# An attention block's forward and backward on one core: V scaled instead of K, whole 12 KB rows for V, column tiles, and score sums on the tensor engine

## Chip, cores and metric

One core of a Trainium2 chip. The metric is device time in microseconds (us) of one execution. PE is the tensor engine (matmuls), PEld its weight loads, DVE the vector engine, ACT the scalar engine, POOL and SP the two engines that issue most transfers.

## The reference

A block with one query token, 32 heads of width 192 and caches of 8192 keys and values per head, all in bf16: an adaptive layer norm, attention over the caches, an output projection, then an MLP. Forward and the gradients of it are wanted. What matters here:

```python
q = (x @ wq).reshape(B, Sq, Hq, Dh)                      # one token, Hq = 32, Dh = 192
scores = einsum('bhqd,bhkd->bhqk', q, k) * Dh ** -0.5    # 8192 keys a head
p = softmax(scores)
o = einsum('bhqk,bhkd->bhqd', p, v)
# ... output projection, MLP ...
out, vjp = jax.vjp(f, x, k_cache, v_cache, wq, wo, ...)  # the outputs include dK and dV, as large as the caches
```

K and V are 100 MB each (32 x 8192 x 192 x 2 bytes), and so are dK and dV. K is read once, V twice.

## The kernel before

Three stages. The **forward** goes through the heads; in step i it computes the scores of head i (multiply K by q, fold the 192 columns, sum) and, for head i-1 whose exponentials E are known, the matrix M = sum over keys of E * K^T [1, V], 194 columns wide. M gives o and the softmax sum Z, and spares the backward a second reading of K. K is scaled by E, in quarters of 16 key columns. V lies in a padded buffer: a column pair of keys has two columns of ones before and after it. A **middle** does the MLP. The **backward** reads V again: per half head it makes dP = V do (multiply, fold, sum), from it dS, and writes dV = E do^T (matmuls with one row, copied out by ACT) and dK = dS q^T.

J = 64 keys a partition, JH = 32, JQ = 16.

```python
    def load_v(h, t):
        vb = VB[nv[0] % NVB]
        nv[0] += 1
        nc.sync.dma_start(out=vb[:, :, 2 : 2 + PW], in_=V_hd[h][:, t * JH : (t + 1) * JH, :].rearrange("p (a b) d -> p a (b d)", b=2))
        return vb

    def dot_half(src4, vec, dst):
        prod = pp.tile([P, JH, DH], BF16, name="prod", tag="prod")
        V_.tensor_tensor(
            out=prod.rearrange("p (a b) d -> p a b d", b=2),
            in0=src4,
            in1=vec[:, None, None, :].to_broadcast([P, JH // 2, 2, DH]),
            op=ALU.mult,
        )
        w = DH
        for _ in range(3):
            w //= 2
            V_.tensor_tensor(out=prod[:, :, 0:w], in0=prod[:, :, 0:w], in1=prod[:, :, w : 2 * w], op=ALU.add)
        V_.reduce_sum(out=dst, in_=prod[:, :, 0:w], axis=AX.X)
# ... cut ...
        def scale_k(q, kb, E4, Ef):
# ... cut ...
            A_.copy(out=ks[:, :, DH:KW], in_=E4[:, j0 : j0 + JQ, :])
            V_.tensor_tensor(
                out=ks[:, 0:n, 0:DH].rearrange("p j (a b) -> p j a b", b=4),
                in0=kb[:, k0 : k0 + n, :].rearrange("p j (a b) -> p j a b", b=4),
                in1=E4[:, j0 : j0 + n, None, :].to_broadcast([P, n, DH // 4, 4]),
                op=ALU.mult,
            )
# ... cut ...
        def m_quarter(q, ks, vb, mp):
            for k in range(JQ):
                s = q == 0 and k == 0
                e = q == 3 and k == JQ - 1
                a, b = divmod((q % 2) * JQ + k, 2)
                o = 2 * b
                rhs = vb[:, a, b * (DH + 2) : b * (DH + 2) + DH + 2]
                T_.matmul(mp[:, o : o + DH + 2], lhsT=ks[:, k * KW : k * KW + P], rhs=rhs, start=s, stop=e, skip_group_check=True)
                T_.matmul(mp[:, MO + o : MO + o + DH + 2], lhsT=ks[:, k * KW + P : k * KW + 2 * P], rhs=rhs, start=False, stop=e, skip_group_check=True)
# ... cut ...
            for t in range(2):
                if i < HQ:
                    dot_half(kh[t].rearrange("p (a b) d -> p a b d", b=2), qs_bc[:, i * DH : (i + 1) * DH], S_h[:, t * JH : (t + 1) * JH])
                if i > 0:
                    pk, pv, pE4, pEf = st[i - 1]
                    for q in (2 * t, 2 * t + 1):
                        ks = scale_k(q, pk[t], pE4, pEf)
                        m_quarter(q, ks, pv[t], mp)
                if i < HQ and t == 0:
                    vh.append(load_v(i, 1))
            if i < HQ:
                E4, Ef = softmax(i, S_h)
                st[i] = (kh, vh, E4, Ef)
# ... cut ...
            for t in range(2):
                js = slice(t * JH, (t + 1) * JH)
                v = load_v(h, t)
                dP = tcol(JH, "dP")
                dot_half(v[:, :, 2 : 2 + PW].rearrange("p a (b d) -> p a b d", b=2), doh, dP)
# ... cut ...
                dSf = tcol(NAK, "dSf")
                A_.copy(out=dSf, in_=dS4[:, 0:NAK, 0])
                dK = ob.tile([P, JH, DH], BF16, name="dK", tag="o")
                for jj in range(NAK):
                    A_.activation(out=dK[:, jj, :], in_=qh, func=ACT.Copy, scale=dSf[:, jj : jj + 1])
                times(dK, qh, dS4, NAK, JH)
                nc.gpsimd.dma_start(out=dK_hd[h][:, js, :], in_=dK)
```

`pp`, the pool of `prod`, has one buffer. The code gives the order in which instructions are written; the programming layer's scheduler decides in which order each engine issues them, and that can differ.

Of the kernel before, what the change touches and what calls it, by code (L numbers as in the profile page):

```python
# [8 lines left out]
FP32 = mybir.dt.float32  # L9
BF16 = mybir.dt.bfloat16  # L10
# [10 lines left out]
def kernel(  # L21
# [35 lines left out]
    JQ = J // 4  # L57
    ND = D // P
# [5 lines left out]
    VP = PW + 4  # L64
    KW = DH + 4
    MW = DH + 4
    SCALE = DH ** -0.5
    assert DH == 192 and HQ % 2 == 0 and J % 4 == 0
    assert D % P == 0 and F % P == 0 and NMOD % PW == 0
# [5 lines left out]
    wst = ctx.enter_context(tc.tile_pool(name="wst", bufs=3))  # L75
    vp = ctx.enter_context(tc.tile_pool(name="vp", bufs=1))
# [4 lines left out]
    psT = ctx.enter_context(tc.tile_pool(name="psT", bufs=1, space=PS))  # L81
    psX_cm = tc.tile_pool(name="psX", bufs=1, space=PS)
    psX = psX_cm.__enter__()
    psO_cm = tc.tile_pool(name="psO", bufs=1, space=PS)
    psO = psO_cm.__enter__()
    psM_cm = tc.tile_pool(name="psM", bufs=2, space=PS)
    psM = psM_cm.__enter__()
# [10 lines left out]
    ones_f = const.tile([P, P], FP32, name="ones_f")  # L98
    V_.memset(ones_f, 1.0)
# [8 lines left out]
    V_.memset(omask, 1.0)  # L108
    V_.memset(omask[:, 0, 1:2], 0.0)
    V_.memset(omask[:, 2, 0:1], 0.0)  # L110
    V_.memset(omask[64:128, 1, 0:1], 0.0)
    V_.memset(omask[0:64, 1, 1:2], 0.0)
# [64 lines left out]
    wo_v = A_wo.rearrange("(c p) r -> p c r", p=P)  # L177
    dwq_v = out_4.rearrange("(i p) n -> p i n", p=P)
    dwo_v = out_5.rearrange("(c p) r -> p c r", p=P)
# [6 lines left out]
    def load_w(view3, lo):  # L186
        w = wst.tile([P, ND, PW], BF16, name="w_st", tag="w")
        nc.sync.dma_start(out=w, in_=view3[:, :, lo : lo + PW])
        return w

    def load_wo(t):
        w = wst.tile([P, 3, D], BF16, name="wo_st", tag="w")
        nc.sync.dma_start(out=w, in_=wo_v[:, 3 * t : 3 * t + 3, :])
        return w
# [24 lines left out]
    def mod_chunk(g, w):  # L219
        ps = psS.tile([P, 4], FP32, name="mod_ps", tag="s")  # L220
        for b in range(3):
            for k in range(ND):
                T_.matmul(ps[:, b : b + 1], lhsT=w[:, k, b * P : (b + 1) * P], rhs=sc_bf[:, k : k + 1], start=(k == 0), stop=(k == ND - 1))
        A_.copy(out=mod[:, 3 * g : 3 * g + 3], in_=ps[:, 0:3])

    sa, ca, ga, sb, cb, gb = (mod[:, k * ND : (k + 1) * ND] for k in range(6))
    NG0 = (2 * ND + 2) // 3
    wm0 = [load_w(wm_v, g * PW) for g in range(NG0)]
    n0, r0 = layernorm(x_c, "ln0")
    for g in range(NG0):  # L230
        mod_chunk(g, wm0[g])
# [8 lines left out]
    def q_pair(t, w):  # L240
        ps = psB.tile([P, 512], FP32, name="q_ps", tag="b")
        for k in range(ND):
            T_.matmul(ps[:, 0:PW], lhsT=ha_bf[:, k : k + 1].to_broadcast([P, P]), rhs=w[:, k, :], start=(k == 0), stop=(k == ND - 1))
        A_.activation(out=qs_bc[:, t * PW : (t + 1) * PW], in_=ps[:, 0:PW], func=ACT.Copy, scale=SCALE)
# [12 lines left out]
    NVB = 3  # L257
    VB = []
    for b in range(NVB):
        vb = vp.tile([P, JH // 2, VP], BF16, name=f"VB{b}")  # L260
        V_.memset(vb[:, :, 0:2], 1.0)
        V_.memset(vb[:, :, VP - 2 : VP], 1.0)
        VB.append(vb)
    nv = [0]

    def load_v(h, t):
        vb = VB[nv[0] % NVB]
        nv[0] += 1
        nc.sync.dma_start(out=vb[:, :, 2 : 2 + PW], in_=V_hd[h][:, t * JH : (t + 1) * JH, :].rearrange("p (a b) d -> p a (b d)", b=2))
        return vb  # L270

    def dot_half(src4, vec, dst):
        prod = pp.tile([P, JH, DH], BF16, name="prod", tag="prod")
        V_.tensor_tensor(  # L274
            out=prod.rearrange("p (a b) d -> p a b d", b=2),
# [504 lines left out]
```

## Time and profile before

1653.24 us (median of 3 runs, 1652.61 to 1654.24). I divide the profiled run by three marks in the trace: the start of the last head's exponential, the start of the first dS, and the end.

| | kernel before |
|---|---|
| first / last exponential | 34.2 / 703.1 us |
| time per head between them | 21.58 us |
| middle (last exponential to first dS) | 77.5 us |
| backward (first dS to end, 1647.8 us) | 867.2 us |

The table of windows, kernel before: per stretch the busy us of each engine with its number of instructions, then PE's granted clock (1 is full), the share of time that the 16 DMA engines were busy, and GB/s.

```profile
...
core 0: us, PE busy (x) PEld busy (x) DVE busy (x) ACT busy (x) POOL busy (x), PEclk, DMA share, GB/s
200.00:400.00 200.00, 142.47 (x1408) 131.68 (x1406) 186.66 (x175) 103.66 (x328) 0.00 (x0) 0.80 0.93 319
400.00:600.00 200.00, 144.78 (x1452) 134.73 (x1450) 187.75 (x172) 100.94 (x317) 0.00 (x0) 0.82 0.93 318
1000.00:1200.00 200.00, 88.61 (x766) 38.24 (x764) 165.35 (x201) 130.54 (x234) 23.60 (x38) 0.52 1.04 387
1200.00:1400.00 200.00, 90.17 (x788) 39.34 (x788) 164.00 (x189) 133.80 (x238) 22.69 (x37) 0.51 1.03 389
...
```

In the forward DVE is busy 186.66 of 200 us. The transfers are at a share of 0.93. In the backward the transfers are saturated (1.03 to 1.04) at under 390 GB/s.

The waits view of DVE, forward (200 to 600 us): instruction and line, what it waited for, us in total, times, longest.

```profile
...
DVE negm L315 <- PE mx L313: 11.2, 11, 1.7
DVE prod L274 <- ACT qs_bc L244: 5.6, 7, 1.4
...
```

Hardly anything: 374.41 us of DVE work over 18.5 heads is 20.2 us a head, and the waits add little over one. The same view in the backward (950 to 1600 us):

```profile
...
DVE prod L274 <- DMA VB_238<-in_A_v_cache_dram: 75.5, 8, 15.0
DVE prod L274 <- DMA VB_241<-in_A_v_cache_dram: 17.5, 5, 9.6
DVE prod L274 <- DMA VB_244<-in_A_v_cache_dram: 10.1, 1, 10.1
...
```

There DVE waits for V. The transfer part of the page tells why V is slow:

```profile
...
DMA packets 349978, 575.64 MB, mean 349 GB/s; under 512 B 9998, under 2 KB 319246, under 8 KB 325294
...
q1 hardware_dynamic: 322538, 347.23, 63.2%
...
```

Most packets are under 2 KB: V's padded buffer takes 768-byte pieces, 41 ns each in the trace (19 GB/s an engine), while K's 12,288-byte rows take 473 ns (26 GB/s).

### The profile page before, as it was taken

What the parts mean: (1) busy time and instruction counts of PE and PEld (TensorE: products, weight loads), DVE (VectorE), ACT (ScalarE), POOL (GpSimd) and SP (SyncE); (2) the same over time, 40 slices, a digit from 0 to 9 for tenths busy, and PEclk for the clock granted to TensorE, in tenths of its full rate; (3) what the DMA queues carried; (4) which work ended last, traced back from release to release, by engine and by line L of the source; (5) the groups of instructions that cost most, each with busy time, mean ns of one, the idle gap of its engine ahead of it and who ended that gap; (6) DMA issues with size and microseconds to landing.
All of it is one profiled execution on the core that took longest, in us unless ns stands there. A gap on an engine that the chain in (4) does not pass through costs nothing.

```text
span 1647.8 us, 22572 instructions
## 1 busy us (share of the span) xinstructions
PE 914.9 (56%) x8675; PEld 650.6 (39%) x8675; DVE 1401.1 (85%) x1590; ACT 952.9 (58%) x2193; POOL 113.7 (7%) x190
## 2 busy tenths in 40 slices
PE   2777767676777767774654343535444335353422
PEld 2666656676766666663321121212121112121100
DVE  6898899999999999955979797969779778797977
ACT  2445544464555555553886575748676657476655
POOL 0000000000000000001111111101101101110110
PEclk9777777888787888775555555555555555555555
DMA  9899889999999999884999999999999999999997
GB/s 339 304 335 300 304 313 319 327 320 336 311 333 304 331 320 335 287 272 158 393 397 390 383 404 380 392 379 398 382 388 398 382 386 390 385 395 385 404 384 329
DMA packets 349978, 575.64 MB, mean 349 GB/s; under 512 B 9998, under 2 KB 319246, under 8 KB 325294
## 3 DMA queue, kind: packets, MB, share of 16 engines
q1 hardware_dynamic: 322538, 347.23, 63.2%
q0 software_dynamic: 24496, 225.92, 32.7%
q8 instruction: 68, 1.11, 0.3%
q10 hardware_dynamic: 2836, 1.05, 0.2%
q14 instruction: 40, 0.33, 0.1%
HBM read 347.74 MB, written 226.43 MB: 348 GB/s over the span
## 4 chain that ended last, share of the span: by engine, by line
DVE 43%; DMA 33%; PE 14%; issue 6%; ACT 3%; SPq 0%; POOL 0%; ACTq 0%; POOLq 0%; DVEq 0%
DMA VB_238<-in_A_v_cache_dram 17%; DVE prod L274 14%; DVE prod L283 12%; DMA VB_241<-in_A_v_cache_dram 8%; PE mp L348 5%; PE mp L349 5%; DVE dK L685 5%; DMA VB_244<-in_A_v_cache_dram 4%; DVE S_h L284 2%; DVE KS_264 L331 2%; DVE KS_266 L331 2%; DMA w_st<-in_A_wq_dram 1%; DMA wo_st<-in_A_wo_dram 1%; DVE KS_262 L331 1%; DVE dP L284 1%
## 5 line engine op out<-in xcount | busy, mean ns | idle before, releaser
L680 PE MATMUL dv_ps<-do_bc,er_b 1*128 1x192 bf16 x2048 | 254.2, 341 | 348.4 <-ACT dV L681 347.7
L283 DVE TENSOR_TENSOR prod<-prod 128x3072 bf16<-128x3072 bf16 (+2 forms) x384 | 416.8, 1085 | 3.8
L681 ACT CAST dV<-dv_ps 128x768 bf16<-128x768 f32 x512 | 365.6, 805 | 4.6 <-PE dv_ps L680 4.4
L680 PEld LDWEIGHTS <-er_b 1*128 1x128 bf16 x2048 | 68.9, 102 | 519.6 <-issue 518.6
L274 DVE TENSOR_TENSOR prod<-VB_238,do_bc 128x6144 bf16<-128x6144 bf16 x21 | 70.4, 3355 | 86.3 <-DMA VB_238<-in_A_v_cache_dram 86.3
L740 ACT ACTIVATE dK<-qs_bc,dSf 128x192 bf16<-128x192 bf16 x320 | 117.6, 445 | 1.6
L353 ACT COPY M_232<-mp 128x196 f32<-128x196 f32 x32 | 10.3, 322 | 167.8 <-PE mp L349 167.8
L348 PE MATMUL mp<-VB_238,KS_262 128*128 128x194 bf16 x352 | 83.1, 296 | 20.1 <-DVE KS_262 L331 20.1
L348 PE MATMUL mp<-VB_244,KS_264 128*128 128x194 bf16 x336 | 74.9, 286 | 28.5 <-DVE KS_264 L331 28.5
L274 DVE TENSOR_TENSOR prod<-VB_241,do_bc 128x6144 bf16<-128x6144 bf16 x22 | 73.7, 3351 | 19.9 <-DMA VB_241<-in_A_v_cache_dram 17.5
L274 DVE TENSOR_TENSOR prod<-VB_244,do_bc 128x6144 bf16<-128x6144 bf16 x21 | 70.4, 3351 | 20.8 <-DMA VB_244<-in_A_v_cache_dram 20.7
L348 PE MATMUL mp<-VB_241,KS_266 128*128 128x194 bf16 x336 | 74.6, 285 | 22.7 <-DVE KS_266 L331 22.7
L348 PEld LDWEIGHTS <-KS_264 128*128 128x128 bf16 x688 | 72.6, 106 | 34.1 <-DVE KS_264 L331 32.4
L348 PEld LDWEIGHTS <-KS_262 128*128 128x128 bf16 x688 | 74.1, 108 | 28.4 <-DVE KS_262 L331 26.7
L349 PE MATMUL mp<-VB_238,KS_262 128*128 128x194 bf16 x352 | 82.9, 295 | 0.9 <-ACT KS_262 L330 0.9
L348 PEld LDWEIGHTS <-KS_266 128*128 128x128 bf16 x672 | 70.4, 105 | 29.8 <-DVE KS_266 L331 28.4
L349 PEld LDWEIGHTS <-KS_262 128*128 128x128 bf16 x688 | 75.2, 109 | 2.8 <-ACT KS_262 L330 1.2
L742 POOL DMA_DIRECT2D out_dram<-dK x64 | 34.7, 542 | 583.5 <-ACT dV L681 373.7
L349 PE MATMUL mp<-VB_244,KS_264 128*128 128x194 bf16 x336 | 74.5, 284 | 0.2 <-ACT KS_264 L330 0.2
L349 PE MATMUL mp<-VB_241,KS_266 128*128 128x194 bf16 x336 | 74.2, 283 | 0.2 <-ACT KS_266 L330 0.2
L349 PEld LDWEIGHTS <-KS_264 128*128 128x128 bf16 x688 | 73.6, 107 | 1.7 <-ACT KS_264 L330 0.4
L349 PEld LDWEIGHTS <-KS_266 128*128 128x128 bf16 x672 | 71.4, 106 | 1.5 <-ACT KS_266 L330 0.4
(898 smaller groups left out, 2300.5 us busy)
## 6 DMA issues: line engine op xcount, KB each, us to landing
out_dram<-dV POOLq DMA_DIRECT2D x64, 1536.0 KB, 11.9
out_dram<-dK POOLq DMA_DIRECT2D x64, 1536.0 KB, 9.0
VB_238<-in_A_v_cache_dram SPq DMA_DIRECT2D x43, 1536.0 KB
VB_241<-in_A_v_cache_dram SPq DMA_DIRECT2D x43, 1536.0 KB
VB_244<-in_A_v_cache_dram SPq DMA_DIRECT2D x42, 1536.0 KB
KB_258<-in_A_k_cache_dram SPq DMA_DIRECT2D x13, 1536.0 KB
KB_259<-in_A_k_cache_dram SPq DMA_DIRECT2D x13, 1536.0 KB
KB_260<-in_A_k_cache_dram SPq DMA_DIRECT2D x13, 1536.0 KB
```

The source lines that it names most:

```text
L274: V_.tensor_tensor(out=prod.rearrange("p (a b) d -> p a b d", b=2), in0=src4, in1=vec[:, None, None, :].to_broadcast([P, JH // 2, 2, DH]), ...
L283: V_.tensor_tensor(out=prod[:, :, 0:w], in0=prod[:, :, 0:w], in1=prod[:, :, w : 2 * w], op=ALU.add)
L284: V_.reduce_sum(out=dst, in_=prod[:, :, 0:w], axis=AX.X)
L331: V_.tensor_tensor(out=ks[:, 0:n, 0:DH].rearrange("p j (a b) -> p j a b", b=4), in0=kb[:, k0 : k0 + n, :].rearrange("p j (a b) -> p j a b" ...
L348: T_.matmul(mp[:, o : o + DH + 2], lhsT=ks[:, k * KW : k * KW + P], rhs=rhs, start=s, stop=e, skip_group_check=True)
L349: T_.matmul(mp[:, MO + o : MO + o + DH + 2], lhsT=ks[:, k * KW + P : k * KW + 2 * P], rhs=rhs, start=False, stop=e, skip_group_check=True)
L353: A_.copy(out=M1[:, h, :], in_=mp[:, 0:MW])
L680: T_.matmul(ps[:, b, k * DH : (k + 1) * DH], lhsT=er[p0 : p0 + 1, 2 * m + k, :], rhs=doh[p0 : p0 + 1, :], start=True, stop=True)
L681: A_.copy(out=dV4[:, 2 * q : 2 * q + 2, m * PW : (m + 1) * PW], in_=ps[:, :, 0:PW])
L685: V_.tensor_tensor(out=out3[:, n0_:n1_, :].rearrange("p j (a b) -> p j a b", b=4), in0=vec.rearrange("p (a b) -> p a b", b=4)[:, None, :, ...
L740: A_.activation(out=dK[:, jj, :], in_=qh, func=ACT.Copy, scale=dSf[:, jj : jj + 1])
L742: nc.gpsimd.dma_start(out=dK_hd[h][:, js, :], in_=dK)
```

## The change

Intent: V arrives in whole 12 KB rows, unpadded. So V instead of K is scaled by E, K goes into the matmuls raw, and M is made in three passes over 16 keys: 128 columns of K in one full-width matmul each; its last 64 columns in tiles of 64 columns, two keys side by side; o and Z by a matrix of ones in tiles of 32 columns, four keys side by side. Because DVE was full, two of three foldings and the sum's width are taken off it: the product is summed by identity matmuls that accumulate in PSUM (6 per half head in the forward, after one folding; 12 in the backward, after none), and DVE sums the last 16 columns. Weights come in chunks twice as wide, with one buffer instead of three, and dK is made by DVE alone.

```diff
     def load_v(h, t):
-        vb = VB[nv[0] % NVB]
-        nv[0] += 1
-        nc.sync.dma_start(out=vb[:, :, 2 : 2 + PW], in_=V_hd[h][:, t * JH : (t + 1) * JH, :].rearrange("p (a b) d -> p a (b d)", b=2))
# ... cut ...
+        v = vp.tile([P, JH, DH], BF16, name="v_sb")
+        nc.sync.dma_start(out=v, in_=V_hd[h][:, t * JH : (t + 1) * JH, :])
+        return v
+
+    def dot_mul(src, vec, halve, psR):
+
         prod = pp.tile([P, JH, DH], BF16, name="prod", tag="prod")
-        V_.tensor_tensor(
-            out=prod.rearrange("p (a b) d -> p a b d", b=2),
-            in0=src4,
-            in1=vec[:, None, None, :].to_broadcast([P, JH // 2, 2, DH]),
-            op=ALU.mult,
-        )
+        V_.tensor_tensor(out=prod, in0=src, in1=vec[:, None, :].to_broadcast([P, JH, DH]), op=ALU.mult)
         w = DH
-        for _ in range(3):
+        if halve:
             w //= 2
             V_.tensor_tensor(out=prod[:, :, 0:w], in0=prod[:, :, 0:w], in1=prod[:, :, w : 2 * w], op=ALU.add)
-        V_.reduce_sum(out=dst, in_=prod[:, :, 0:w], axis=AX.X)
+        ps = psR.tile([P, JH, TS], FP32, name="dot_ps")
+        for k in range(0, w, TS):
+            T_.matmul(ps, lhsT=ident_bf, rhs=prod[:, :, k : k + TS], start=(k == 0), stop=(k == w - TS))
+        return ps
+
+    def dot_sum(ps, dst):
+        V_.reduce_sum(out=dst, in_=ps, axis=AX.X)
 
# ... cut ...
-        def m_quarter(q, ks, vb, mp):
+                A_.activation(out=vs[:, k, 0:DH], in_=v[:, v0 + k, :], func=ACT.Copy, scale=Ef[:, j0 + k : j0 + k + 1])
+            return vs
# ... cut ...
+        def m_quarter(q, kb, vs, mp, op):
+            j0 = (q % 2) * JQ
+            z = q == 3
             for k in range(JQ):
-                s = q == 0 and k == 0
# ... cut ...
+                T_.matmul(mp[:, 0:MW], lhsT=kb[:, j0 + k, 0:P], rhs=vs[:, k, 0:MW], start=(q == 0 and k == 0), stop=(z and k == JQ - 1), skip_group_check=True)
+
+            for k in range(JQ):
+                p0 = 64 * (k % 2)
+                T_.matmul(mp[p0 : p0 + 64, MO : MO + MW], lhsT=kb[:, j0 + k, P:DH], rhs=vs[:, k, 0:MW], start=False, stop=(z and k >= JQ - 2), skip_group_check=True)
+
+            for k in range(JQ):
+                p0 = 32 * (k % 4)
+                T_.matmul(op[p0 : p0 + 32, 0:MW], lhsT=ones_bf, rhs=vs[:, k, 0:MW], start=(q == 0 and k < 4), stop=(z and k >= JQ - 4), skip_group_check=True)
+
# ... cut ...
+                    wo_l[i // 2] = load_wo(i // 2)
+            if old:
+                pk, pv, pE4, pEf = st.pop(i - 1)
+                mp = psM.tile([P, 512], FP32, name="mp")
+                op = psO.tile([P, 256], FP32, name="op")
+
+            def quarter(q):
+                if old:
+                    m_quarter(q, pk[q // 2], scale_v(q, pv[q // 2], pE4, pEf), mp, op)
+
+            if new:
+                d0 = dot_mul(kh[0], qh, True, psR)
+            quarter(0)
+            if new:
+                d1 = dot_mul(kh[1], qh, True, psR)
+                dot_sum(d0, S_h[:, 0:JH])
+            quarter(1)
+            if new:
+                vh.append(load_v(i, 1))
+                dot_sum(d1, S_h[:, JH:J])
                 E4, Ef = softmax(i, S_h)
                 st[i] = (kh, vh, E4, Ef)
```

```diff
-                dot_half(v[:, :, 2 : 2 + PW].rearrange("p a (b d) -> p a b d", b=2), doh, dP)
-                dS4 = bst.tile([P, JH, 4], BF16, name="dS4")
+                dot_sum(dot_mul(v, doh, False, psR), dP)
+                dS4 = bst.tile([P, JH, 4], BF16, name="dS4", bufs=2)
                 V_.scalar_tensor_tensor(
                     out=dS4,
# ... cut ...
-                dSf = tcol(NAK, "dSf")
-                A_.copy(out=dSf, in_=dS4[:, 0:NAK, 0])
                 dK = ob.tile([P, JH, DH], BF16, name="dK", tag="o")
-                for jj in range(NAK):
-                    A_.activation(out=dK[:, jj, :], in_=qh, func=ACT.Copy, scale=dSf[:, jj : jj + 1])
-                times(dK, qh, dS4, NAK, JH)
+                times(dK, qh, dS4, 0, JH)
                 nc.gpsimd.dma_start(out=dK_hd[h][:, js, :], in_=dK)
                 for f in side.get(2 * h + t, ()):
```

Cut marks stand for the weight chunks, the outputs of a head, PSUM pools and the MLP's pools.

## The prediction

> **What bounds it now.** Forward (to about 725 us), middle (to 785), backward (to 1648). The table of windows gives, forward: DVE 93% busy, DMA share 0.93, PE clock 0.8; backward: DMA share 1.04 at 390 GB/s, DVE 84%, clock 0.5. Forward, DVE and DMA both bind: heads start 21.6 us apart (exp to exp in the timeline, 34.2 to 703.1 us); about 20 us is DVE work. Backward, DMA binds: the waits view shows DVE waiting 125 us for V loads, one half head takes 13.4 us. Cause, from the packets: V comes in 768-byte packets of 41 ns (19 GB/s an engine), K in 12,288-byte ones of 473 ns (26 GB/s); 0.0375 ns a byte plus 12 ns a packet. The Trainium skill, "DMA: Bandwidth & Descriptors" (Why small descriptors are slow), states a fixed cost per packet; the trace agrees, with 12 ns.
>
> **DMA.** V as 12 KB rows: 131,072 packets of 41 ns become 8,192 of 473 ns, saving about 94 us of all 16 engines forward and 80 us backward. Wider weight rows save about 8 us in each. Per head forward 20 us becomes about 16; per half head backward 13.4 becomes 12.0.
>
> **DVE.** Forward per head it loses two of three foldings (0.87 and 0.47 us net, twice), has a shorter sum (0.95 to an estimated 0.7, 512 fp32 from PSUM), and slightly less scaling: 20 us becomes about 16.3. But `prod` has one buffer: the second multiply must wait until TensorE has read the first product (6 matmuls of 512 columns, about 1.3 us full clock, plus latency and the ones pass queued ahead: about 1.9 us); the last sum waits about 1.2 us; the max broadcast 0.4; exp 0.7. Sum 20.5 to 20.9 us a head, against 21.6. DVE's saving mostly turns into waits for PE. Backward DVE drops from 10.3 to about 7.6 us a half head plus side work, and does not bind.
>
> **PE.** Forward 64 full, 64 half-width and 64 quarter-width matmuls per head. The skill, "TensorEngine Tiling (Array Packing)" (Key Properties), says tiles run in parallel and a mode switch drains. The trace agrees: transposes with 64 columns start in pairs 0 to 4 ns apart, one pair per 106 ns; going to or from the 128-wide mode adds about 135 ns (half clock). A quarter costs about 1.33+0.66+0.33+0.4 = 2.7 us, 11 a head, with the sums about 15. If they ran one by one it would be 16 us plus drains, and forward would slow to over 24 us a head. Backward 12 matmuls of 512 columns per half (2.6 us, or 5.1 at clock 0.5) interleave with outer products and drains: chain sum, multiply, PE about 9.5 us at full clock, 13 at half. I expect a clock of 0.6-0.8, so DMA mostly binds.
>
> **Sum.** Forward -20 us (-45 to +25), middle -4, backward 860 to about 805 (-55; -80 to -10). Time about 1578 us, range 1515 to 1650. Faster by over 2% 0.77, within 2% 0.18, slower 0.05.
>
> **Would show it.** DMA share forward about 0.8; DVE idle forward mostly before the second multiply and the sums, released by PE; half- and quarter-width matmuls starting in groups; backward V waits shrinking, DMA share still near 1.
>
> **Would break it.** Column tiles not concurrent, or costlier drains; backward clock staying 0.5, so the sums hold dK back; V loads stuck behind weight loads (one weight buffer) in the in-order SP queue; or TensorE sums nearly free, giving 1515.

## The result

1715.82 us (median of 4 runs, 1714.61 to 1722.23) against 1653.74 (1652.61 to 1655.24, 4 runs): ratio 1.0383, 95% interval 1.0355 to 1.0411. Ratios here and below are the mean time of one kernel's fast runs over that of the kernel before in the same rounds, so not quite the ratio of the quoted medians. The change was slower, where 1578 us had been predicted.

| stage | before | after | difference |
|---|---|---|---|
| time per head | 21.58 | 23.53 | +1.95 |
| last exponential | 703.1 | 763.7 | +60.6 |
| middle | 77.5 | 87.5 | +10.0 |
| backward | 867.2 | 861.6 | -5.6 |
| span | 1647.8 | 1712.8 | +65.0 |

The windows of the kernel after, same columns:

```profile
...
200.00:400.00 200.00, 163.85 (x1874) 110.49 (x1872) 137.27 (x128) 105.26 (x331) 0.00 (x0) 0.82 0.73 289
400.00:600.00 200.00, 166.23 (x2025) 114.12 (x2025) 142.65 (x132) 109.69 (x344) 0.00 (x0) 0.88 0.74 298
1000.00:1200.00 200.00, 161.43 (x1055) 59.73 (x1054) 134.50 (x183) 116.13 (x159) 21.68 (x38) 0.60 1.00 402
1200.00:1400.00 200.00, 153.16 (x906) 50.89 (x905) 130.31 (x155) 109.68 (x151) 19.26 (x34) 0.58 0.99 402
...
```

DVE fell from 187 to about 140 us of 200, and the DMA share to 0.74, as intended. But fewer heads fit in. The waits of DVE in the forward, after:

```profile
...
DVE prod L266 <- PE dot_ps L273: 66.7, 17, 5.3
DVE S_h L277 <- PE dot_ps L273: 25.0, 18, 2.4
DVE negm L302 <- PE mx L300: 12.0, 17, 0.9
DVE vs L316 <- ACT vs L323: 6.5, 7, 1.4
...
```

From 200 to 600 us there are 17 heads: 279.92 us of DVE work is 16.5 us a head (predicted 16.3), and the waits are 7.1 us a head (predicted 4.2). The first line alone, the second multiply waiting for PE to have read the first product, is 66.7 / 17 = 3.9 us; 1.9 was predicted. In the backward one wait took the place of V's:

```profile
...
DVE dP L277 <- PE dot_ps L273: 198.0, 48, 15.8
...
```

The transfers did become cheaper:

```profile
...
DMA packets 78270, 576.00 MB, mean 336 GB/s; under 512 B 9374, under 2 KB 27118, under 8 KB 37182
...
q1 hardware_dynamic: 51530, 347.23, 51.2%
...
```

349,978 packets became 78,270, and the loads' share fell from 63.2% to 51.2% of the span.

One head of the kernel after shows the wait. The timeline of DVE: start, us, instruction, and in brackets how long the engine had been idle and who ended that.

```profile
...
463.32 3.00 DVE L316 TENSOR_TENSOR vs<-v_sb,E_5709 128x1728 bf16<-128x1728 bf16 x3 [0.58 <-ACT E_5709 L304]
466.23 3.35 DVE L266 TENSOR_TENSOR prod<-KB_241,qs_bc 128x6144 bf16<-128x6144 bf16 x1
470.58 1.06 DVE L316 TENSOR_TENSOR vs<-v_sb,E_5709 128x1728 bf16<-128x1728 bf16 x1 [1.00 <-ACT vs L323]
471.55 1.75 DVE L270 TENSOR_TENSOR prod<-prod 128x3072 bf16<-128x3072 bf16 x1
477.49 3.36 DVE L266 TENSOR_TENSOR prod<-KB_237,qs_bc 128x6144 bf16<-128x6144 bf16 x1 [4.19 <-PE dot_ps L273]
```

All four scalings of the old head stand before the new head's fold (three at 463.32, the last at 470.58); the product is folded by 473.30, and the next thing in DVE's order is the second multiply. PE at that time:

```profile
...
473.39 1.52 PE L330 MATMUL mp<-vs,KB_240 128*128 128x193 bf16 x16
474.84 0.86 PE L334 MATMUL mp<-vs,KB_240 128*64 128x193 bf16 x16
475.62 0.43 PE L338 MATMUL op<-vs,ones_bf 128*32 128x193 bf16 x11
475.99 1.47 PE L273 MATMUL dot_ps<-prod,ident_bf 128*128 128x512 bf16 x6
...
```

The six score matmuls (dot_ps) start only at 475.99: PE has 16, 16 and 11 matmuls of the old head's third quarter to do first, because they stand ahead in its queue. DVE multiplies again at 477.49, after 4.19 us of idling. The other heads look the same: over the 22 heads between 130 and 640 us, the first half's score matmuls start 2.64 us on the mean after their product is folded, PE is busy with other matmuls all that time, and the six take 1.46 us. The page "Perfetto Trace Analysis" of the Trainium skill (Tensor Engine Instruction) says that PE reorders in a limited way, pulling weight loads ahead of matmuls in flight; that is no help for a matmul, and the trace agrees: the score matmuls started only after the old head's, 2.7 us after their input was ready.

### The profile page after: what moved, and what is told of

Same layout as the page of the kernel before. It is cut to its first block, busy times and chain, and to the rows that moved or that the text cites. A ratio compares the mean times of both kernels' runs of the same rounds, so it can differ in the third digit from the quotient of the medians.

```text
span 1712.8 us, 28289 instructions
## 1 busy us (share of the span) xinstructions
PE 1311.6 (77%) x11811; PEld 675.5 (39%) x11811; DVE 1114.0 (65%) x1273; ACT 900.0 (53%) x1948; POOL 99.9 (6%) x177
## 2 busy tenths in 40 slices
DMA packets 78270, 576.00 MB, mean 336 GB/s; under 512 B 9374, under 2 KB 27118, under 8 KB 37182
## 3 DMA queue, kind: packets, MB, share of 16 engines
q1 hardware_dynamic: 51530, 347.23, 51.2%
q10 hardware_dynamic: 2836, 1.05, 0.2%
## 4 chain that ended last, share of the span: by engine, by line
PE 40%; issue 23%; DVE 14%; DMA 12%; ACT 7%; POOL 2%; SPq 0%; POOLq 0%; ACTq 0%; DVEq 0%
PE dot_ps L273 14%; PE mp L330 10%; DVE prod L266 7%; DMA v_sb<-in_A_v_cache_dram 4%; PE mp L334 4%; PE op L338 3%; PE dv_ps L682 3%; ACT vs L323 3%; DVE prod L270 3%; DMA w_st<-in_A_wq_dram 2%; ACT dV L683 2%; PE wT_ps L573 2%; DMA wo_st<-in_A_wo_dram 2%; DMA w_st<-in_w_mod_dram 1%; DVE S_h L277 1%
## 5 line engine op out<-in xcount | busy, mean ns | idle before, releaser
L273 PE MATMUL dot_ps<-prod,ident_bf 128*128 128x512 bf16 x1152 | 475.0, 542 | 87.1 <-DVE prod L270 46.6
L323 ACT ACTIVATE vs<-v_sb,Ef 128x192 bf16<-128x192 bf16 x896 | 325.8, 448 | 0.0
L273 PEld LDWEIGHTS <-ident_bf 128*128 128x128 bf16 x1152 | 119.4, 117 | 264.7 <-issue 233.9
L266 DVE TENSOR_TENSOR prod<-v_sb,do_bc 128x6144 bf16<-128x6144 bf16 x64 | 214.3, 3349 | 3.5 <-ACT do_bc L624 3.5
L270 DVE TENSOR_TENSOR prod<-prod 128x3072 bf16<-128x3072 bf16 x64 | 112.0, 1750 | 0.0
L338 PE MATMUL op<-vs,ones_bf 128*32 128x193 bf16 x2048 | 102.6, 264 | 0.0
L573 PE MATMUL wT_ps<-ident_bf,w_st 128*128 128x128 bf16 (+1 forms) x470 | 50.7, 285 | 66.4 <-ACT wqT L574 25.8
L574 ACT COPY wqT<-wT_ps 128x1024 bf16<-128x1024 bf16 (+1 forms) x52 | 50.6, 973 | 49.2 <-PE wT_ps L573 35.1
L741 POOL DMA_DIRECT2D out_dram<-dV x64 | 35.4, 553 | 658.2 <-ACT dV L683 635.1
L266 DVE TENSOR_TENSOR prod<-KB_238,qs_bc 128x6144 bf16<-128x6144 bf16 x13 | 43.6, 3355 | 28.8 <-PE dot_ps L273 23.9
L266 DVE TENSOR_TENSOR prod<-KB_241,qs_bc 128x6144 bf16<-128x6144 bf16 x13 | 43.6, 3356 | 27.4 <-PE dot_ps L273 27.4
L266 DVE TENSOR_TENSOR prod<-KB_239,qs_bc 128x6144 bf16<-128x6144 bf16 x13 | 43.6, 3356 | 27.3 <-PE dot_ps L273 27.3
L330 PE MATMUL mp<-vs,KB_238 128*128 128x193 bf16 x416 | 52.6, 275 | 10.6 <-DVE vs L316 6.3
L330 PE MATMUL mp<-vs,KB_240 128*128 128x193 bf16 x416 | 52.3, 275 | 10.6 <-DVE vs L316 8.4
```

What stands on the lines that cost most here:

```text
L266: V_.tensor_tensor(out=prod, in0=src, in1=vec[:, None, :].to_broadcast([P, JH, DH]), op=ALU.mult)
L273: T_.matmul(ps, lhsT=ident_bf, rhs=prod[:, :, k : k + TS], start=(k == 0), stop=(k == w - TS))
L323: A_.activation(out=vs[:, k, 0:DH], in_=v[:, v0 + k, :], func=ACT.Copy, scale=Ef[:, j0 + k : j0 + k + 1])
L330: T_.matmul(mp[:, 0:MW], lhsT=kb[:, j0 + k, 0:P], rhs=vs[:, k, 0:MW], start=(q == 0 and k == 0), stop=(z and k == JQ - 1), skip_group_chec ...
L338: T_.matmul(op[p0 : p0 + 32, 0:MW], lhsT=ones_bf, rhs=vs[:, k, 0:MW], start=(q == 0 and k < 4), stop=(z and k >= JQ - 4), skip_group_check ...
L573: T_.transpose(out=tp[lo:hi, (x - x0) * P : (x - x0 + 1) * P], in_=src, identity=ident_bf)
```

## The experiments

| run | last exponential | middle | backward | median us | ratio |
|---|---|---|---|---|---|
| before | 703.1 | 77.5 | 867.2 | 1653.74 | 1 |
| after | 763.7 | 87.5 | 861.6 | 1715.82 | 1.0383 |
| e1 two product buffers | 737.0 | 84.7 | 897.3 | 1716.44 | 1.0362 |
| e2 forward sums on DVE | 702.2 | 87.7 | 865.0 | 1657.09 | 1.0009 |
| e3 backward sums on DVE | 765.9 | 84.6 | 854.0 | 1707.31 | 1.0312 |
| e4 all sums on DVE | 702.4 | 84.7 | 854.9 | 1645.43 | 0.9944 |
| e5 few ones matmuls (wrong) | 744.2 | 86.9 | 865.2 | 1697.88 | 1.0254 |
| e6 two folds, two products | 720.0 | 89.5 | 827.2 | 1638.55 | 0.9905 |
| e7 = e4, two products | 687.0 | 88.9 | 831.6 | 1610.26 | 0.9727 |
| e8 before, forward sums on PE | 727.2 | 81.0 | 869.0 | 1682.60 | 1.0161 |
| e9 = e4, more weight buffers | 703.8 | 84.4 | 807.8 | 1598.24 | 0.9656 |
| e10 after, forward order fixed | 658.2 | 87.8 | 861.9 | 1605.46 | 0.9695 |
| e11 = e9, two products forward | 688.3 | 82.2 | 807.6 | 1580.22 | 0.9550 |
| e12 = e10's forward, e9's backward | 652.1 | 83.6 | 807.7 | 1543.90 | 0.9330 |
| e13 = e12, forward sums on DVE | 765.1 | 83.4 | 817.8 | 1662.69 | 1.0041 |

Two more runs, d1 and d2, cut the backward to its transfers and are told below. All but d1, d2 and e5 gave correct results.

### Whose loss is it: e1 to e4

**e1_two_products**: `prod` gets a second buffer (M1 goes to bf16 to make room).

```diff
-    pp = ctx.enter_context(tc.tile_pool(name="pp", bufs=1))
+    pp = ctx.enter_context(tc.tile_pool(name="pp", bufs=2))
-    M1 = const.tile([P, HQ, MW], FP32, name="M1")
+    M1 = const.tile([P, HQ, MW], BF16, name="M1")
```

> After the change, with two product buffers instead of one (room for it comes from keeping the K-side sums M1 in bf16). Theory: forward is slow because the second multiply of a head waits until TensorE has read the first product (99 us of waits between 100 and 700 us, about 4 us each time), as there is one buffer. Then this wait goes to near 0, heads go from 23.5 to about 20.5 us, and the time from 1716 to about 1620. Rival: TensorE is overloaded by the three passes and their mode switches, and DVE would wait elsewhere (before the sums): heads stay at 23 us or more, time within 1% of 1716.

The forward gained 27 us but stayed at 22.77 us a head, and the backward lost 36. DVE's waits fell only from 7.1 to 6.2 us a head: they moved to the sums (1.8) and to the scaling, which waited for ACT (2.2). The theory's 20.5 us and 1620 us were missed; the time is within 1% of the change's, as the rival had it, though a head took a little less than its 23 us. So the single buffer is where the wait showed, and at most a part of its cause. Why the backward lost 36 us was not looked into.

**e2_fwd_sums_dve**, **e3_bwd_sums_dve**, **e4_all_sums_dve**: the sums go back to DVE with three foldings, in the forward, in the backward, or in both; the rest of the change stays.

```diff
-                d0 = dot_mul(kh[0], qh, True, psR)          # e2, e4
+                dot_half(kh[0], qh, S_h[:, 0:JH])
-                d1 = dot_mul(kh[1], qh, True, psR)
-                dot_sum(d0, S_h[:, 0:JH])
+                dot_half(kh[1], qh, S_h[:, JH:J])
-                dot_sum(d1, S_h[:, JH:J])
-                dot_sum(dot_mul(v, doh, False, psR), dP)    # e3, e4
+                dot_half(v, doh, dP)
```

> After the change, with the forward score sums back on DVE (three foldings and a sum over 24, as before), everything else as after. Theory (TensorE sums put TensorE into DVE's chain): DVE work per head rises from about 16 to 19.5 us, its waits for TensorE nearly vanish, heads take about 21 us instead of 23.5, time about 1635. Rival (TensorE overloaded by the three passes, or ACT's seven scalings a quarter): heads stay at 23 us or more although 12 of the 204 matmuls are gone, time 1700 or more.

> After the change, with the backward sums back on DVE, everything else as after. Theory: backward the chain sum, multiply, 12 matmuls cut up by outer products at half clock (12.3 us at the end of the trace, 13.4 on the mean) holds every half head; with DVE sums the half head falls to what DMA and DVE allow, about 12.2 us, time about 1645, and DVE waits for V loads come back. Rival: DMA is at its limit backward anyway (share 0.97 to 1.0, 402 GB/s): backward stays at 860 us, time within 0.7% of 1716.

> After the change, with all score sums back on DVE: the layout of V and the weights, V scaled, and the column tiles alone. Theory: both gains add, heads 21 us and half heads 12.2 us, time about 1565 to 1590, faster than before by 4 to 5%. Rival (column tiles and mode switches, or ACT, to blame): time stays over 1653.

The forward's loss of 61 us goes with the sums on PE, all of it: without them e2's last exponential is at 702.2 us against 703.1 before. That also says what the faster V transfers were worth in the forward: nothing, as the DMA share fell to 0.80 and the time stayed, because DVE was the bound (0.92 busy from 100 to 650 us, before 0.93). In the backward, the sums on PE cost 8 us against DVE's (e3). e4, with the change's transfers and no sums on PE, is 0.9944. The expected sizes were missed: e2 reached 1657 us instead of 1635, e3 1707 instead of 1645 (where its rival had put it) and e4 1645 instead of 1565 to 1590, so something else held the backward up.

### The transfers by themselves: d1 and d2

**d1_before_dma_only** and **d2_after_dma_only**: in the backward of each kernel the half head is cut to its load, its two stores and one-element copies that tie them together. The results are wrong; the weight work stays.

```diff
+                for o_, out_hd in ((OB[(2 * ni[0]) % 4], dV_hd), (OB[(2 * ni[0] + 1) % 4], dK_hd)):
+                    V_.tensor_copy(out=o_[:, 0, 0:1], in_=v[:, 0, 0:1])
+                    nc.gpsimd.dma_start(out=out_hd[h][:, js, :], in_=o_)
# ... dP, dS, dV and dK removed ...
```

> The kernel before with the backward loop cut to its transfers (wrong dK and dV on purpose): each V half is loaded, one column of two ready tiles is copied from it, and those are stored as dV and dK; the weight side work stays. It measures what the DMA of the backward stretch costs by itself with V in 768-byte packets. If DMA bound the stretch before, it stays near 860 us (389 GB/s). If the coupling of the engines did, it falls well below 830.

> The changed kernel cut in the same way: V in 12,288-byte packets. As predicted (each 768-byte packet costs its 12 ns beside its bytes, 80 us in all): the stretch takes 765 to 790 us, 70 or more less than the same cut of the kernel before. Rival (the core's data rate with loads and stores mixed stops near 400 GB/s whatever the packets, since two queues hide each other's fixed cost): it takes 830 or more and lies within 20 us of the other cut.

The times were 1650.51 us (ratio 0.9968) and 1686.89 us (1.0188). d1's backward, from its first store to the end, took 865.8 us at 390 GB/s, as long as the whole kernel's: the backward before was bound by its transfers alone. d2's took 835.3 us, 30 us less, so both of its expectations missed (70 or more; under 20). In ten of the last twenty slices of the span it moved 422 to 431 GB/s, with slices down to 342 between:

```profile
...
GB/s 349 331 306 293 259 315 243 292 288 332 294 283 286 290 307 328 293 275 196 106 332 386 350 427 403 365 415 342 427 427 429 427 431 345 416 422 424 428 425 365
...
```

Its waits view (900 to 1600 us) has ACT's broadcast vector waiting 372 us for DVE to have done with the staged gradient before it. That alone explains nothing: d1 has the same wait, 393.9 us, with its transfers saturated. So the gain of the whole rows is real, and why a transfer bound near 335 MB / 427 GB/s = 785 us (an estimate from d2's good slices) is not reached stays open here; e9 below tries the single weight buffers. The Trainium skill, "DMA: Bandwidth & Descriptors" (Where 436 GB/s comes from), puts the ceiling at 435 GB/s for the ports but says that the memory's side, about 358 a core (a stack's rate divided between two cores), binds between HBM and SBUF; here one core, alone in its program, moved 427 with loads and stores mixed (d2), so the measurement decides for the higher figure.

### Is it PE's load or the sums: e5, e6, e8

**e5_few_ones**: 44 of 64 ones matmuls per head are left out.

```diff
-            for k in range(JQ):
+            for k in range(JQ) if z else range(4) if q == 0 else ():
```

> After the change, with only 20 of the 64 ones matmuls of a head (wrong o and Z on purpose), so two of four ones passes with their mode switches are gone and one is cut to four. Theory (the first sums' matmuls stand in TensorE's in-order queue behind the passes of the third quarter, and DVE waits for them): the wait before the second multiply falls from 3.9 us a head by 1 to 1.5 us, heads from 23.5 to about 22 us. Rival (TensorE's half clock at the start of each head or the latency of the sums themselves is to blame, not the queue): heads change by less than 0.5 us.

The forward gained 20 us, 22.90 us a head, and the share of time at full clock fell from 0.70 to 0.57. The multiply's wait fell by 0.6 us a head, the head by 0.63: both expectations missed, and since the clock fell too, e5 does not tell the queue from the clock. Less work on PE helped, but neither restored the time nor removed the waits (6.5 us a head).

**e6_two_folds_two_products**: two foldings and three matmuls per half in the forward, two product buffers, backward sums on DVE.

```diff
-        if halve:
+        for _ in range(2 if halve else 0):
-                dot_sum(dot_mul(v, doh, False, psR), dP)
+                dot_half(v, doh, dP)
```

> After the change, forward with two foldings on DVE and 3 instead of 6 matmuls a sum, two product buffers (M1 in bf16); backward sums on DVE. Theory (forward: DVE's work plus its waits for TensorE make the head): DVE work about 18.3 us, waits about 2.3 us, heads about 20.6 us against 21.6 with all sums on DVE; time about 1615 to 1625, faster than both kernels. Rival (any sum on TensorE costs as much wait as it saves work): heads 21.6 or more, time 1645 or more.

The forward's last exponential came at 720.0 us, 22.22 us a head where the theory had 20.6, still later than with no sums on PE. The backward took 827 us where e4's, with the same code but one product buffer, took 855; that raised a new question (e7).

**e8_before_fwd_sums_pe**: the kernel before, with only its forward sums moved to PE.

```diff
+        w = DH // 2
+        V_.tensor_tensor(out=prod[:, :, 0:w], in0=prod[:, :, 0:w], in1=prod[:, :, w : 2 * w], op=ALU.add)
+        for k in range(0, w, 16):
+            T_.matmul(dp[:, t * JH : (t + 1) * JH, :], lhsT=ident_bf, rhs=prod[:, :, k : k + 16], start=(k == 0), stop=(k == w - 16))
# ... one reduce_sum over 16 columns per half, as in the change; K scaled and V padded as before ...
```

> The kernel before with one part of the change alone: the forward score sums on the tensor engine (one halving, six identity matmuls per half, a last sum over 16 columns), K scaled and V padded as before, one product buffer as before. Theory A (the loss of the forward comes from putting the sums behind the products of K and V in the tensor engine's in-order queue, whatever the form of those products): 22.5 to 24 us a head, last exponential at 735 to 770 us against 703, time 1685 to 1720 us. Rival B (the three passes with column tiles make the queue slow, and the sums alone would pay): 20 to 21 us a head, last exponential at 655 to 690 us, time 1605 to 1640 us.

The windows of e8's forward and the waits of its DVE (200 to 600 us):

```profile
...
200.00:400.00 200.00, 163.71 (x1472) 138.67 (x1471) 151.16 (x133) 97.58 (x312) 0.00 (x0) 0.86 0.88 303
400.00:600.00 200.00, 164.62 (x1484) 140.73 (x1483) 149.95 (x129) 99.72 (x319) 0.00 (x0) 0.88 0.89 306
...
```

```profile
...
DVE prod L288 <- PE dot_ps L297: 41.7, 18, 2.8
DVE S_h L424 <- PE dot_ps L297: 21.3, 18, 1.6
...
```

DVE's work fell as it did in the change (301.11 against 374.41 us in these 400 us), and the same two waits came in its place. The last exponential came at 727.2 us, 24 us late, under the range that the queue theory had given (735 to 770), but on its side and far from the rival's. So neither V's scaling nor the column tiles are needed for the loss; they make it larger. In e8 the first half's score matmuls start 0.83 us after their product (the change: 2.64), all of it PE's other matmuls, and take 1.46 us: here their own time is the larger part of the wait.

### The order of the queue: e10 and e13

An old head has 3 passes x 64 = 192 matmuls on PE. In the kernel's text a new head's score matmuls come before the first of them and after 48. In the built program of the change, counted over heads 1 to 31, those of the first half stand behind 106 to 156 of the 192, and those of the second half behind all 192: the scheduler put the scalings together, and the score matmuls where it took them to be ready. Only the first half's are delayed by what stands ahead; the second half's start 0.08 us after their product, the old head's being done by then. In e10 they stand behind 0 and 48, as in the text. **e10_fwd_order_fixed** fixes the order in which DVE and PE issue the forward loop.

```diff
+        ordered.enter_context(tc.manual_schedule(engines={mybir.EngineType.DVE, mybir.EngineType.PE}))
 ...
             if new:
                 d0 = dot_mul(kh[0], qh, True, psR)
             quarter(0)
# ... cut: outputs of the head before the old one (copies, add, po matmuls; chunks of q or mod) ...
             if new:
                 d1 = dot_mul(kh[1], qh, True, psR)
-                dot_sum(d0, S_h[:, 0:JH])
             quarter(1)
# ... cut: second part of those outputs ...
             if new:
+                dot_sum(d0, S_h[:, 0:JH])
                 dot_sum(d1, S_h[:, JH:J])
-                E4, Ef = softmax(i, S_h)
+                mx = head_max(S_h)
             quarter(2)
             quarter(3)
+            if new:
+                E4, Ef = softmax(i, S_h, mx)
```

Loads of the q and mod weights are issued a step earlier, so that PE's fixed order does not wait for them. Work and buffers are those of the change.

> The changed kernel with one thing altered: in the forward loop the vector and tensor engines issue in an order fixed by hand instead of the scheduler's. Scheduler's order: all four scalings of the old head back to back, then multiply and halving of both halves of the new head, so that the second half's score matmuls stand behind the whole fourth quarter of passes. Fixed order: each half's multiply and halving alternate with one scaling, both sums stand after the second scaling, and the outputs of a finished head are taken up one quarter into the next. Work, buffers and transfers are the same. Theory Q (the forward's loss is the position of the score matmuls in the tensor engine's in-order queue): the second multiply waits under 1.5 us a head instead of 4.0, heads of 18 to 21.5 us, last exponential at 595 to 700 us, time 1545 to 1650 us. Rival T (the tensor engine has too much work a head at the clock it gets, 19.5 us of busy time with all waits inside, so any order costs the same): heads of 22.5 us or more, last exponential at 730 us or later, time over 1675 us.

1605.46 us, ratio 0.9695 (0.9656 to 0.9733); the last exponential is at 658.2 us, 105 us earlier than in the change, 20.15 us a head. All of it is in the forward: middle and backward are the change's to half a microsecond. Windows and waits of its forward:

```profile
...
200.00:400.00 200.00, 169.48 (x2149) 124.56 (x2149) 160.61 (x147) 116.70 (x369) 0.00 (x0) 0.84 0.85 331
400.00:600.00 200.00, 171.55 (x2322) 128.91 (x2319) 166.50 (x155) 125.61 (x396) 0.00 (x0) 0.91 0.89 346
...
```

```profile
...
DVE prod L266 <- DMA KB<-in_A_k_cache_dram: 31.0, 14, 7.3
DVE S_h L277 <- PE dot_ps L273: 21.1, 16, 2.4
DVE negm L305 <- PE mx L300: 18.9, 19, 2.1
DVE prod L266 <- PE dot_ps L273: 5.5, 9, 1.5
...
```

The first line of the change's list, 66.7 us, is now the last, 5.5 us. In its place stands a wait for K, with the DMA share at 0.85 to 0.89, perhaps the next limit (not tested). PE is as busy as in the change (170 of 200 us against 165), with more heads done; rival T, by which any order costs the same, has fallen. A head now keeps PE busy for 17.2 us instead of 19.4, at full clock for 0.76 of these 400 us instead of 0.70. Whether this is a part of the gain or comes of it no run tells. PE's timeline shows how the score matmuls now stand between quarters:

```profile
...
464.64 0.52 PE L341 MATMUL op<-vs,ones_bf 128*32 128x193 bf16 x16
465.27 1.46 PE L273 MATMUL dot_ps<-prod,ident_bf 128*128 128x512 bf16 x6
...
468.80 0.52 PE L341 MATMUL op<-vs,ones_bf 128*32 128x193 bf16 x16
472.87 2.72 PE L273 MATMUL dot_ps<-prod,ident_bf 128*128 128x512 bf16 x6 [3.56 <-DVE prod L270]
475.39 2.79 PE L333 MATMUL mp<-vs,KB 128*128 128x193 bf16 x16
...
```

At 465.27 and 472.87 six score matmuls follow whole passes. The second group had to wait 3.56 us for DVE, which had itself waited 1.10 us for K, and it took 2.72 us instead of 1.46: the trace's clock record is at 0.5 from 471.6 for 6.8 us. The Trainium skill, "TensorE: Matmul & The Clock Gate" (What's actually happening), tells of a clock that is either full or half, and half after an idle window of about 3.4 us; this trace agrees in that it shows only 0.5 and 1.0, and half-clock periods that are multiples of 3.4 us, but PE had not idled through the 3.4 us before 471.6: it had stopped at 469.3.

e10 changes the order on two engines, and with it when outputs are taken up. The trace ties the gain to the score matmuls: the second multiply's wait for them fell by 3.6 us a head, the time by 3.4. Of the 3.6, about 2.6 are PE's queue (the score matmuls' delay fell from 2.64 to 0.05 us); the other 1 us is the length of the scaling (1.05 us) that DVE now does between the fold and the second multiply, while PE reads the product. This split is an estimate from the traces; the parts were not run one by one.

**e13_fixed_order_dve_sums** asks whether a fixed order is good by itself: e12 (below) with the forward's sums on DVE.

```diff
-                d0 = dot_mul(kh[0], qh, True, psR)
+                dot_half(kh[0], qh, S_h[:, 0:JH])
-                d1 = dot_mul(kh[1], qh, True, psR)
+                dot_half(kh[1], qh, S_h[:, JH:J])
-                dot_sum(d0, S_h[:, 0:JH])
-                dot_sum(d1, S_h[:, JH:J])
```

> e12_fixed_order_e9_backward with the forward's score sums put back on the vector engine, in the same hand-fixed order; beside e12 it tells what the move of the sums itself is worth once the order is right. If the move is worth the 3.7 us less vector-engine work a head that the traces show, cut to what the vector engine bounds: heads near 21 us (20 us of vector-engine work), last exponential at 680 to 695 us against 652, time 1570 to 1590 us. If e10's whole gain came from the order whatever does the sums: last exponential at 645 to 660 us, time 1535 to 1550 us.

Both expectations missed: 23.63 us a head, last exponential at 765.1 us, 1662.69 us in all. The wait that grew is that for the maximum, whose PE matmul stands in front of the third quarter but behind the second:

```profile
...
DVE negm L314 <- PE mx L309: 50.7, 16, 4.3
...
```

So a fixed order as such gains nothing. This one fits sums on PE, and spoils the kernel with sums on DVE, for which the scheduler's order is better (e9, whose work and buffers e13 has: 703.8). It also means that e13 does not say what the sums are worth in an order good for both; the fairest comparison is each in the better order that was tried, 688.3 (e11, DVE) against 652.1 us (e12, PE).

### The backward: e7, e9, e11, e12

**e7_all_sums_dve_two_products**: e4 with e6's two product buffers and bf16 M1 (the edit of e1).

> The changed kernel with all score sums back on the vector engine (as in e4_all_sums_dve) and, in addition, the two product buffers and bf16 M1 of e6_two_folds_two_products. e6's stage after the middle took 827 us with exactly the vector-engine sums for which e4 took 855 us. Theory A (the second product buffer, or the smaller M1, is worth it, since the next half's multiply no longer waits behind the last reader): last exponential at 700 to 705 us, backward 825 to 835 us, time 1615 to 1625 us. Theory B (with vector-engine sums writer and readers of the product are one in-order engine, so a second buffer can change nothing, and e6's 827 us came from how its forward left queues and clock): backward 850 to 858 us, time 1640 to 1648 us.

The backward took 831.6 us, so e6's gain came with these two edits. The forward gained 15 us as well, which theory A had not foreseen. In the forward's trace the foldings of the two halves alternate in most heads, which one buffer forbids; DVE's work per head is the same. That the order does it, and not the buffer in another way, was not tested. (e11 below differs from e9 by the second buffer alone and gains the same 15 us, so the forward's gain is not that of the bf16 M1.)

**e9_more_weight_buffers**: e4 with a second buffer each for the wide weight chunk, its staged gradient and the broadcast vector (M1 and M2 in bf16 to make room).

```diff
-                cur["w"] = load_w(view, lo, lo + CW)
+                nw[0] += 1
+                if nw[0] % 2:
+                    cur["w"] = load_w(view, lo, lo + CW)
+                else:
+                    cur["w"] = bst.tile([P, ND, CW], BF16, name="w2_st")
+                    nc.sync.dma_start(out=cur["w"], in_=view[:, :, lo : lo + CW])
-                cur["stg"] = bst.tile([P, ND, CW], BF16, name="stg")
+                cur["stg"] = bst.tile([P, ND, CW], BF16, name="stg", bufs=2)
-            v_bc = bst.tile([P, PW], BF16, name="v_bc")
+            v_bc = bst.tile([P, PW], BF16, name="v_bc", bufs=2)
```

> e4_all_sums_dve (all sums on the vector engine, one product buffer) with M1 and M2 in bf16, and the backward's weight work loosened: two buffers for the wide weight chunks, two for their staged gradients, two for the broadcast vector. If the single weight buffers hold up the tensor engine and with it the sums and the transfers, as waits of 45 to 75 us on the weight loads and conversions suggest: backward 825 to 840 us against 855 for e4, time 1615 to 1632 us. Rival (the vector engine's work, about 89 per cent busy, or the transfers set the backward whatever the weights do): backward 850 to 857 us, time 1640 to 1650 us.

807.8 us, better than the range. Windows of the backward, first e4, then e9:

```profile
...
1000.00:1200.00 200.00, 99.33 (x841) 41.73 (x841) 180.67 (x211) 116.72 (x165) 22.62 (x39) 0.50 1.00 406
1200.00:1400.00 200.00, 90.31 (x772) 37.46 (x771) 183.93 (x205) 109.52 (x155) 20.92 (x38) 0.51 1.00 405
1400.00:1600.00 200.00, 71.70 (x644) 26.18 (x641) 177.32 (x174) 96.66 (x136) 20.12 (x36) 0.50 0.97 390
...
```

```profile
...
1000.00:1200.00 200.00, 98.72 (x801) 40.78 (x800) 186.72 (x214) 112.49 (x159) 22.00 (x39) 0.51 1.01 424
1200.00:1400.00 200.00, 98.39 (x817) 39.67 (x815) 191.62 (x210) 117.02 (x165) 20.96 (x38) 0.50 1.01 422
1400.00:1550.00 150.00, 61.55 (x531) 21.80 (x529) 142.11 (x140) 80.47 (x113) 17.50 (x31) 0.50 1.00 416
...
```

and what PE waited for beside its outer products (950 to 1550 us), first e4, then e9:

```profile
...
PE acc_ps L596 <- DVE v_bf L591: 73.1, 10, 10.8
PE wT_ps L580 <- DMA w_st<-in_w_mod_dram: 43.5, 3, 17.1
...
```

```profile
...
PE acc_ps L596 <- DVE v_bf L591: 13.4, 5, 6.1
...
```

The wait for the weight chunk (43.5 us) is gone from e9's list and the conversion's fell from 73.1 to 13.4. The transfers run at 416 to 424 GB/s with a share of 1.0, near d2's best rate. But DVE is fuller than in e4 (93 to 96%), and it no longer waits for V; its longest wait in these 600 us is

```profile
...
DVE dha L597 <- PE acc_ps L596: 16.1, 6, 4.6
...
```

while the loads of V wait for DVE to have multiplied an earlier half (322.7 us of SP's waits from 950 to 1500 us). So e9's backward is held by DVE's work at least as much as by its transfers. Which of the two ends it first, and which of the three buffers mattered, was not told apart.

**e11_fwd_two_products_dve**: e9 with a second product buffer in the forward only, from a pool that is freed before the backward.

```diff
+        npr[0] += 1
+        if p2[0] is not None and npr[0] % 2 == 0:
+            prod = p2[0].tile([P, JH, DH], BF16, name="prod2")
+        else:
+            prod = pp.tile([P, JH, DH], BF16, name="prod", tag="prod")
```

> e9_more_weight_buffers with a second product buffer in the forward alone (all sums stay on the vector engine). e7's forward ended at 687 us against 702 to 704 for the same work with one buffer; with two the scheduler interleaves the folds of the two halves. If the gains add: last exponential at 684 to 692 us, backward 805 to 812 us, time 1578 to 1588 us. If e7's forward gain was not the buffer: last exponential at 700 to 705 us, time 1594 to 1602 us.

688.3 and 807.6 us, 1580.22 in all: the two gains add.

**e12_fixed_order_e9_backward**: e10's forward with e9's backward.

> e10's forward (score sums on the tensor engine, hand-fixed order) with e9's backward (sums on the vector engine, more weight buffers). If the two stages are independent, the last exponential is e10's and the backward e9's 808 us: under theory Q 1490 to 1595 us, under rival T 1620 us or more.

1543.90 us (1540.09 to 1547.39), ratio 0.9330 (0.9310 to 0.9349). The stages are independent: 652.1 us and 807.7 us. It beats both kernels, by 6.7% and by 10% (1543.90 / 1715.82 = 0.900).

## Why the prediction was wrong

- **What bounds the kernel: partly right.** The backward was transfer-bound (d1 shows it). In the forward, "DVE and DMA both bind" was wrong: with the change's transfers and DVE sums, the DMA share fell to 0.80 and the last exponential moved by 1 us (e2). DVE, 0.92 to 0.93 busy in both, bound alone, so the estimate of about 94 us saved by V's packets bought nothing there.
- **DVE's work: right.** 16.5 us a head, predicted about 16.3.
- **The step that failed: DVE's waits for PE.** The prediction had the second multiply wait "about 1.9 us", six matmuls plus "the ones pass queued ahead", and 4.2 us of waits in all. Measured: 3.9 and 7.1 us. The six matmuls were nearly right (1.46 us for 1.3); the term that failed is what is queued ahead of them, 2.6 us on the mean instead of about 0.6. The prediction had one pass ahead of the first half's matmuls; in the built program these stand behind 106 to 156 of the old head's 192 matmuls, and the example head had 43, most of three passes, to go when the product was ready. e8 shows that waits for PE come with the sums alone, e1 that a buffer mostly moves them, and e10 that the order on both engines takes the multiply's wait away (0.3 us): with it a head takes 20.15 us, below the 20.5 to 20.9 that were predicted.
- **Column tiles: right.** Pairs of 64-column tiles start 3 to 4 ns apart and groups of four 32-column tiles as well; a quarter took 2.7 to 3.0 us at full clock (predicted 2.7).
- **PE's clock in the forward: not asked.** Much of the forward ran at half clock (0.30 of it, 0.39 before), where passes and score matmuls take twice as long (a full-width matmul starts every 161 ns instead of 83, a score matmul every 427 instead of 216); the sum was made at full clock.
- **Backward: right about the transfers, wrong about reaching them.** 805 us was predicted and 861.6 measured; e9 reaches 807.8. Two things stood between: PE's chain of sums at a clock of 0.53 to 0.60 (predicted 0.6 to 0.8; waits of 198 us in the list above), and single weight buffers, which the prediction named as a risk for V's loads; they held up PE and ACT instead. Taking only the sums off PE gave 8 us (e3), adding the buffers another 47 (e4 to e9). With the sums back on DVE that engine is nearly full, so e9's 807.8 is not the predicted 805 reached in the predicted way.
- **Middle: wrong sign, +10 instead of -4 us.** The first of the MLP's loads was issued later after the last exponential than before (15.5 against 10 us, from the trace), ahead of a serial chain. No run tested it.

Open: why two product buffers with sums on DVE speed up both stages (e7) and with sums on PE slow the backward (e1), and how much of e10's gain is PE's order, DVE's order, the later outputs and the higher clock.

## What to carry to other kernels

When work moves from a full engine to another one, the time can go to where the moved instructions stand in the other engine's queue: read the built order, count what is still to do ahead of them when their input is ready, and if a result is waited for, fix the order before judging the move. A saving in transfers or work counts only in the stage whose bound it is, and single-buffered side work can keep a stage from its transfer rate, as in e4 against e9. Test such parts one at a time: here a change that lost 62 us became a gain of 110 us once the order and the buffers were mended and the backward's sums put back.

## What the Trainium skill lacked or had wrong

- "TensorEngine Tiling (Array Packing)", Key Properties: it says that a change of tiling mode drains the engine, without a figure. Start to start, going from the full-width pass to the 64-column pass took 177 ns instead of 83, so about 95 ns more, at full clock; at half clock about 110 ns more there (273 instead of 161), and about 135 for the transposes of the kernel before (241 instead of 107).
- "DMA: Bandwidth & Descriptors", Where 436 GB/s comes from: it has about 358 GB/s bind between HBM and SBUF, without saying there that this is the share when both cores of a pair stream. This core, alone in its program, moved 424 GB/s over 200 us (e9) and up to 431 in a slice (d2), loads and stores mixed; the page's own table of measured loads, for one core, has 425.
- The same page, Why small descriptors are slow: it gives about 3 cycles of overhead a packet, beside one cycle for each 32 bytes. In the forward before, the packets fit 12 ns each plus 0.0375 ns a byte, so 1.2 ns for 32 bytes, and 12 ns are about 10 such steps, not 3 (an estimate from the fit). 768-byte packets ran at 19 GB/s an engine and 12,288-byte ones at 26, and the backward's transfers went from 390 to 424 GB/s (before to e9).
- "TensorE: Matmul & The Clock Gate", What's actually happening: it puts the half clock down to an idle window of about 3.4 us and does not say how little activity counts as idle: in e10 a half-clock period began at 454.5 us after 3.4 us with 1.4 us of idling in it, the rest one-column and score matmuls.
- No page read here tells what a matmul's place in PE's queue can cost: 2.6 us a head in this case, and fixing the order on PE and DVE together gained 105 us of 1716 (e10 against the change).
